# Packing a softmax bound's small matmuls into column groups, sending the result through DRAM, and moving the surrounding schedule

## The chip, the cores and the metric

The kernel runs on one core of a Trainium2 chip. The time is device time in microseconds; most executions of one kernel agree within 0.3%. Each result is a median over several executions, and ratios compare fast runs with fast runs of the kernel before that were taken in the same rounds on the same chip. The TensorE clock that was granted within a run (1.0 is full speed) is given where it matters.

## The reference

A layer norm over 2048 tokens of width 640 feeds two branches. Branch A is a recurrent attention in four segments of 512 tokens with 32 heads of 20 elements: inside a segment causal softmax attention, and across segments a memory that is read with phi(q) and updated with phi(k). Branch B is a gated feed-forward block. The output is x + A * silu(B).

```python
for s in range(N):                       # N = 4 segments
    logits = einsum('bhqd,bhkd->bhqk', qs, ks) * scale + mask
    a_dot = einsum('bhqk,bhkd->bhqd', softmax(logits), vs)
    a_mem = einsum(phi(qs), M) / (einsum(phi(qs), z) + 1e-6)
    outs.append(g * a_mem + (1 - g) * a_dot)
    M, z = M + einsum(phi(ks), vs), z + sum(phi(ks))
...
h = sigmoid(xn @ w_gate) * (xn @ w_up)   # branch B, on the same xn
return x + (o @ wo) * silu(h @ w_down)
```

## The kernel before

Softmax needs no row maximum here: from each score the kernel subtracts an upper bound, so that no exponent is positive. For query q and head h the bound is the sum over d of |q_d| times the largest |k_d| of the segment. It rides in the score matmul as one more contraction row: KT holds a row of ones beside the 20 rows of K, QT holds minus the bound beside the 20 rows of Q.

The bound itself comes from TensorE. `ik` has, for each of five chunks of 128 feature rows, the values -max|k| placed in the column of their head; `aq` is |q|. Before the change this is done for one half of the heads at a time, so twice in a segment:

```python
    def bound_mm(n, half):
        ik, aq = seg[n]["ik"], seg[n]["aq"]
        cps = ps_d.tile([16, L], F32, name="cps", tag="d")
        for i in range(3):
            nc.tensor.matmul(cps[:], lhsT=ik[:, i, :], rhs=aq[:, i, :], start=(i == 0), stop=(i == 2))
        cb = stg.tile([16, L], BF, name="cb", bufs=2)
        nc.vector.tensor_copy(cb[:], cps[:])
    def bound_dma(n, half, engs):          # SBUF to SBUF, one row per head
        for r in range(4):
            engs[r % len(engs)].dma_start(QT[32 * r + DH:32 * r + E1, 4 * half:4 * half + 4, :],
                                          cb[4 * r:4 * r + 4, :])
    def scores(unit):                      # four heads at once, in four row groups of the array
        for r in range(4):
            for (g, kb, c0, ncol, q0) in unit:
                nc.tensor.matmul(Sps[:, r, c0:c0 + ncol],
                                 lhsT=KT[32 * r:32 * r + E1, g, kb * P:(kb + 1) * P],
                                 rhs=QT[32 * r:32 * r + E1, g, q0:L], ..., tile_position=(32 * r, 0))
```

The rest of the kernel is a loop of slots, 20 to a segment and 21 in the last, numbered from 0 to 80. A slot issues one group of scores, ScalarE's exponential of them, the attention matmuls of the slot before, the planned work of that slot (projections of the next segment, phi, the memory), and as much feed-forward work (`do_gate`, `do_up`, `do_down`) as a running budget asks for. The plan of the next segment's preparation, before:

```python
        for slot, fn, c in [(9, do_K, 0), (10, do_K, 1), (11, do_K, 2), (11, do_Q, 0), (12, do_Q, 1), (13, do_Q, 2),
                            (14, do_Q, 3), (15, do_Q, 4), (16, do_K, 3), (17, do_K, 4)]:
            at(slot, GLU_NS, fn, m, c, nc.vector)
        for i in range(8):
            at(10 + i, V_NS, do_V, m, i // 2, i % 2, nc.scalar)
        ...  # phi of K at 9 to 12, memory update at 13 and 14, bounds at 15 and 19
```

In the prologue, ahead of the first scores, some gate and up pairs stand as filler for TensorE while the first Q, K and bound travel.

## Time and profile before

| | before |
|---|---|
| time, median (range) | 345.98 us (345.58 to 346.6) |
| span of the profiled execution | 344.8 us |
| TensorE busy | 333.9 us, 97% |
| VectorE, ScalarE busy | 222.2, 223.0 us |
| granted clock | 1.0 |

The line of busy times on the profile's page, where PE is TensorE's matmuls, DVE VectorE, ACT ScalarE and POOL GpSimd:

```profile
PE 333.9 (97%) x3386; PEld 184.5 (54%) x3386; DVE 222.2 (64%) x518; ACT 223.0 (65%) x220; POOL 100.8 (29%) x172
```

TensorE is the engine to relieve, and the others have slack on average.

The bound's instructions, from the view of one tile (duration minimum, median, maximum in ns; first and last start):

```profile
L287 PE MATMUL cps<-aq,ik x24: 379/379/383, 23.4 to 254.4; 128*16 128x512 bf16 x24
L289 DVE CAST cb<-cps x8: 669/678/679, 25.1 to 254.8; 16x512 bf16<-16x512 f32 x8
```

A matmul's own duration (379 ns) is not its cost, since matmuls are pipelined. Its cost is how far it pushes the next start. One unit in the loop, from the timeline (start, duration, engine):

```profile
106.99 0.81 PE L287 MATMUL cps<-aq,ik 128*16 128x512 bf16 x3
107.73 0.39 PE L471 MATMUL Sps<-QT,KT 21*128 21x512 bf16 x4
```

The three matmuls push what follows by 0.74 us. The end of the prologue, from the timeline again:

```profile
28.42 0.40 SPq L119 DMA_DIRECT2D xt<-in_A_x_dram  x1
28.93 2.57 SPq L295 DMA_DIRECT2D QT<-cb  x4
...
32.55 1.24 PE L380 MATMUL up<-xnT,Wu 128*128 128x512 bf16 x5
34.45 0.83 PE L471 MATMUL Sps<-QT,KT 21*128 21x512 bf16 x4 [0.65 <-DMA QT<-cb]
35.20 0.60 PE L371 MATMUL gp<-xnT,Wg 128*128 128x512 bf16 x2
```

TensorE waits 0.65 us for the DMA that brings the bound.

### The profile page before, as it was taken

The page shows a single profiled execution, that of the slowest core. Times are in us where ns is not written, and L with a number is a line of the kernel's source. Part 1 is how long each engine was busy: PE and PEld are TensorE (multiplying, and loading weights), DVE is VectorE, ACT ScalarE, POOL GpSimd, SP SyncE. Part 2 cuts the span into 40 slices and gives each one's busy share as a digit, 9 for nine tenths or more (in the row PEclk, how much of TensorE's full clock was granted, in tenths as well). Part 3 has the DMA queues.
Part 4 walks back from the last instruction along what each step waited for, and adds up shares of the span by engine and source line. Part 5 has one row for each costly group of instructions (what it writes and reads, how often), then busy time and mean ns, then how long its engine had stood idle before and what let it go on. Part 6 is the DMA issues. An engine that isn't in the chain of part 4 may idle for free.

```text
span 344.8 us, 8229 instructions
## 1 busy us (share of the span) xinstructions
PE 333.9 (97%) x3386; PEld 184.5 (54%) x3386; DVE 222.2 (64%) x518; ACT 223.0 (65%) x220; POOL 100.8 (29%) x172
## 2 busy tenths in 40 slices
PE   7999999999999999999999999999899999999995
PEld 3543444665554555556566455556456755545663
DVE  5374374375776777798768786878765665543354
ACT  3523676677786866766787667677956767576640
POOL 6800224223222243223232522222322232322203
PEclk9999999999999999999999999999999999999999
DMA  7977784302246614113365324024135000000002
GB/s 225 384 303 209 146 275 145 79 2 84 86 141 138 153 40 128 45 67 107 88 179 144 78 77 99 18 74 133 65 81 153 2 21 21 20 21 2 2 1 76
DMA packets 48965, 35.40 MB, mean 103 GB/s; under 512 B 25248, under 2 KB 47648, under 8 KB 48928
## 3 DMA queue, kind: packets, MB, share of 16 engines
q1 hardware_dynamic: 47616, 30.95, 32.1%
q10 hardware_dynamic: 1312, 3.93, 2.9%
q8 instruction: 26, 0.43, 0.5%
q14 instruction: 11, 0.09, 0.1%
HBM read 17.05 MB, written 11.80 MB: 84 GB/s over the span
## 4 chain that ended last, share of the span: by engine, by line
PE 84%; DVE 6%; ACT 4%; issue 2%; POOL 2%; DMA 1%; SPq 0%; DVEq 0%; ACTq 0%; POOLq 0%
PE yp L394 16%; PE up L380 13%; PE gp L371 13%; PE psq L239 11%; PE Aps L500 8%; PE Sps L471 7%; PE psv L301 5%; PE sp L418 4%; PE am L356 2%; PE cps L287 2%; ACT pt L479 1%; PE sp L452 1%; PE dm L337 1%; DMA QT<-cb 1%; DVE hT L383 1%
## 5 line engine op out<-in xcount | busy, mean ns | idle before, releaser
L479 ACT ACTIVATE pt<-Sps 128x2048 bf16<-128x2048 f32 (+1 forms) x81 | 150.3, 1855 | 36.3 <-PE Sps L471 33.1
L481 POOL TENSOR_SCALAR_AFFINE_SELECT pt<-pt 128x512 bf16<-128x512 bf16 x128 | 81.4, 651 | 227.3 <-ACT pt L479 227.3
L380 PE MATMUL up<-xnT,Wu 128*128 128x512 bf16 x240 | 59.7, 379 | 1.1 <-ACT tg L374 0.9
L371 PE MATMUL gp<-xnT,Wg 128*128 128x512 bf16 x240 | 59.7, 379 | 0.2 <-ACT V L306 0.2
L394 PE MATMUL yp<-Wd,hT 128*128 128x320 bf16 x384 | 57.5, 299 | 0.4 <-ACT oT L437 0.4
L383 DVE SCALAR_TENSOR_TENSOR hT<-tg,up 128x512 bf16<-128x512 bf16 x48 | 32.8, 683 | 37.4 <-PE up L380 27.0
L500 PEld LDWEIGHTS <-pt 128*128 128x128 bf16 x1280 | 42.7, 96 | 14.4 <-issue 3.0
L374 ACT ACTIVATE tg<-gp 128x512 bf16<-128x512 f32 x48 | 28.5, 594 | 26.1 <-PE gp L371 26.1
L500 PE MATMUL Aps<-V,pt 128*128 128x21 bf16 x1280 | 44.6, 173 | 0.0
L394 PEld LDWEIGHTS <-hT 128*128 128x128 bf16 x384 | 35.4, 97 | 15.8 <-issue 3.2
L398 DVE SCALAR_TENSOR_TENSOR aa<-t,yp 128x320 bf16<-128x320 bf16 x32 | 15.6, 488 | 34.0 <-ACT t L397 33.9
L371 PEld LDWEIGHTS <-Wg 128*128 128x128 bf16 x240 | 21.4, 97 | 23.9 <-issue 3.4
L380 PEld LDWEIGHTS <-Wu 128*128 128x128 bf16 x240 | 21.1, 97 | 24.4 <-issue 4.3
L471 PE MATMUL Sps<-QT,KT 21*128 21x128 bf16 (+3 forms) x512 | 32.8, 301 | 1.1 <-DMA QT<-cb 0.7
L301 PE MATMUL psv<-Wv,xnT 128*128 128x320 bf16 x160 | 26.5, 299 | 1.0 <-DVE ktd L244 0.8
L397 ACT ACTIVATE t<-yp 128x320 bf16<-128x320 f32 x32 | 13.9, 435 | 20.3 <-PE yp L394 19.9
L471 PEld LDWEIGHTS <-KT 21*128 21x128 bf16 x512 | 9.7, 92 | 27.6 <-issue 26.6
L239 PE MATMUL psq<-xnT,Wq 128*128 128x512 bf16 x100 | 24.3, 378 | 0.0
L239 PE MATMUL psq<-xnT,Wk 128*128 128x512 bf16 x100 | 24.3, 378 | 0.0
L306 ACT CAST V<-psv 128x320 bf16<-128x320 f32 x32 | 13.7, 427 | 15.0 <-PE psv L301 14.7
L301 PEld LDWEIGHTS <-xnT 128*128 128x128 bf16 x160 | 15.3, 98 | 11.4 <-issue 1.1
L418 PE MATMUL sp<-Wo,oT 128*128 128x320 bf16 x120 | 20.2, 298 | 0.2 <-ACT tg L374 0.2
(81 smaller groups left out, 311.5 us busy)
## 6 DMA issues: line engine op xcount, KB each, us to landing
KT<-Kd SPq DMA_DIRECT2D x32, 80.0 KB
QT<-Qd SPq DMA_DIRECT2D x32, 80.0 KB
out_dram<-xt SPq DMA_DIRECT2D x15, 160.0 KB
Wg<-in_B_w_gate_dram ACTq DMA_DIRECT2D x1, 1920.0 KB
Wu<-in_B_w_up_dram ACTq DMA_DIRECT2D x1, 1920.0 KB
xt<-in_A_x_dram SPq DMA_DIRECT2D x3, 640.0 KB
Wd<-in_B_w_down_dram SPq DMA_DIRECT2D x1, 1920.0 KB
Xd<-xn SPq DMA_DIRECT2D x12, 160.0 KB
```

The costliest lines, as they stand in the source:

```text
L239: nc.tensor.matmul(ps[:], lhsT=W[:, k, c * P:(c + 1) * P], rhs=xnT_of[n][:, k, :], start=(k == 0), stop=(k == DC - 1))
L301: nc.tensor.matmul(ps[:], lhsT=xnT_of[n][:, k, j * P:(j + 1) * P], rhs=Wv[:, k, half * HD:(half + 1) * HD], start=(k == 0), stop=(k == DC ...
L371: nc.tensor.matmul(gp[:], lhsT=Wg[:, k, f * P:(f + 1) * P], rhs=xnT_of[n][:, k, :], start=(k == 0), stop=(k == DC - 1))
L374: nc.scalar.activation(tg[:], gp[:], ACT.Tanh, scale=0.5)
L380: nc.tensor.matmul(up[:], lhsT=Wu[:, k, f * P:(f + 1) * P], rhs=xnT_of[n][:, k, :], start=(k == 0), stop=(k == DC - 1))
L383: nc.vector.scalar_tensor_tensor(out=h[:], in0=seg[n]["tg"][:], scalar=1.0, in1=up[:], op0=ALU.add, op1=ALU.mult)
L394: nc.tensor.matmul(yp[:], lhsT=s["hT"][f][:, j * P:(j + 1) * P], rhs=Wd[:, f, hs], start=(f == 0), stop=(f == FC - 1))
L418: nc.tensor.matmul(sp[:], lhsT=s["oT"][:, c, j * P:(j + 1) * P], rhs=Wo[:, c, hs], start=(c == 0), stop=(c == DC - 1))
L471: nc.tensor.matmul(Sps[:, r, c0:c0 + ncol], lhsT=KT[32 * r:32 * r + E1, g, kb * P:(kb + 1) * P], rhs=QT[32 * r:32 * r + E1, g, q0:L], star ...
L479: nc.scalar.activation(pt[:, :, 0:ntot], Sps[:, :, 0:ntot], ACT.Exp, scale=SCALE)
L481: nc.gpsimd.affine_select(out=pt[:, :, c0:c0 + P], in_=pt[:, :, c0:c0 + P], compare_op=ALU.is_ge, fill=0.0, base=0, pattern=[[0, 4], [1, P ...
L500: nc.tensor.matmul(acc["ps"][:, qb, r, :], lhsT=t[:, r, off:off + P], rhs=V[n % 2][:, kb, 4 * g + r, :], start=acc["fresh"], stop=True, sk ...
```

## The change

The intent is to spend less TensorE time on the bound. All 32 heads are now done in one unit a segment. Each chunk's stationary operand is 128 rows by 32 columns, and chunk c goes to column group c mod 3 of the array, so that three chunks can run side by side. The three column groups leave three partial sums; they are not added, but become three contraction rows of the scores (23 rows in place of 21), where the row of ones adds them. To get three rows per head into QT, the result goes through DRAM.

```diff
-    def bound_mm(n, half):
-        cps = ps_d.tile([16, L], F32, name="cps", tag="d")
-        for i in range(3):
-            nc.tensor.matmul(cps[:], lhsT=ik[:, i, :], rhs=aq[:, i, :], start=(i == 0), stop=(i == 2))
+    def bound_mm(n):
+        cps = ps_d.tile([3 * H, L], F32, name="cps", tag="d")
+        for c in range(DC):
+            i = c % 3
+            nc.tensor.matmul(cps[H * i:H * i + H, :], lhsT=ik[:, c, :], rhs=aq[:, c, :],
+                             start=(c < 3), stop=(c >= 2), tile_position=(0, H * i), skip_group_check=True)
         nc.vector.tensor_copy(cb[:], cps[:])
+        nc.sync.dma_start(Bd[n % 2][:], cb[:])
...
-            engs[r % len(engs)].dma_start(QT[32 * r + DH:32 * r + E1, 4 * half:4 * half + 4, :],
-                                          cb[4 * r:4 * r + 4, :])
+            nc.sync.dma_start(QT[32 * r + DH:32 * r + DH + 3, 4 * half:4 * half + 4, :],
+                              src[r][:, 4 * half:4 * half + 4, :])
...                                   # scores: 32 * r + E1 becomes 32 * r + DH + 3, twice
-    for f in (1, 2):                  # filler pairs after the first one
+    for f in (1, 2, 3):
...
-        for slot, fn, c in [(9, do_K, 0), (10, do_K, 1), (11, do_K, 2), (11, do_Q, 0), (12, do_Q, 1), (13, do_Q, 2),
-                            (14, do_Q, 3), (15, do_Q, 4), (16, do_K, 3), (17, do_K, 4)]:
+        for slot, fn, c in [(9, do_K, 0), (10, do_K, 1), (10, do_K, 2), (11, do_Q, 0), (11, do_Q, 1), (12, do_Q, 2),
+                            (12, do_Q, 3), (13, do_Q, 4), (13, do_K, 3), (14, do_K, 4)]:
-            at(10 + i, V_NS, do_V, m, i // 2, i % 2, nc.scalar)
+            at(12 + i, V_NS, do_V, m, i // 2, i % 2, nc.scalar)
...                                   # phi of K: slots 9-12 become 12-15; memory update: 13, 14 become 17, 18
...                                   # second half of Q spilled at 14, not 16; the bound at 15 and 16
...                                   # prologue: load of the next x issued after the bound's DMA, not before
...                                   # prologue: all K and Q projections ahead of the one bound unit
...                                   # Ind, the constant table that ik is made from: GpSimd builds one of 128x160, not two of 128x48
```

More of the change, by code (lines that the diff above doesn't have):

```diff
@@ L104 @@
     Xd = [dpool.tile([L, D], BF, name=f"Xd{i}") for i in range(2)]
+    Bd = [dpool.tile([3 * H, L], BF, name=f"Bd{i}") for i in range(2)]
     Od = [dpool.tile([L, D], BF, name=f"Od{i}") for i in range(2)]
@@ L151 @@
     nc.gpsimd.memset(KT[:].bitcast(mybir.dt.uint32), 0x3F803F80)
-    Ind = []
-    for hb in range(2):
-        t = cpool.tile([P, 3, 4, 4], F32, name=f"Ind{hb}")
-        nc.gpsimd.memset(t[:], -1.0)
-        base = 2 * hb * P - 16 * hb * DH
-        nc.gpsimd.affine_select(out=t[:], in_=t[:], compare_op=ALU.is_ge, fill=0.0, base=base,
-                                pattern=[[P, 3], [-DH, 4], [-4 * DH, 4]], channel_multiplier=1)
-        nc.gpsimd.affine_select(out=t[:], in_=t[:], compare_op=ALU.is_ge, fill=0.0, base=DH - 1 - base,
-                                pattern=[[-P, 3], [DH, 4], [4 * DH, 4]], channel_multiplier=-1)
-        Ind.append(t)
+    Ind = cpool.tile([P, DC, 4, NG], F32, name="Ind")
+    nc.gpsimd.memset(Ind[:], -1.0)
+    nc.gpsimd.affine_select(out=Ind[:], in_=Ind[:], compare_op=ALU.is_ge, fill=0.0, base=0,
+                            pattern=[[P, DC], [-DH, 4], [-4 * DH, NG]], channel_multiplier=1)
+    nc.gpsimd.affine_select(out=Ind[:], in_=Ind[:], compare_op=ALU.is_ge, fill=0.0, base=DH - 1,
+                            pattern=[[-P, DC], [DH, 4], [4 * DH, NG]], channel_multiplier=-1)
     V = [cpool.tile([P, 4, H, E1], BF, name=f"V{i}") for i in range(2)]
@@ L267, in relayout @@
             eng.dma_start(dst[32 * r:32 * r + DH, 4 * half:4 * half + 4, :], src[r])
-    def bound_q(n, half):
-        aq = stg.tile([P, 3, L], BF, name="aq")
-        U16 = mybir.dt.uint16
-        nc.vector.tensor_scalar(aq[:].bitcast(U16), seg[n]["qt"][:, 2 * half:2 * half + 3, :].bitcast(U16),
-                                0x7FFF, None, op0=ALU.bitwise_and)
-        seg[n]["aq"] = aq
-    def bound_k(n, half):
-        ik = stg.tile([P, 3, 16], BF, name="ik", bufs=2)
-        nc.vector.tensor_tensor(
-            ik[:], Ind[half][:].rearrange("p c r g -> p c (r g)"),
-            seg[n]["kabs"][:, 2 * half:2 * half + 3].unsqueeze(2).to_broadcast([P, 3, 16]), op=ALU.mult)
-        seg[n]["ik"] = ik
@@ L283, in bound_mm, with bound @@
-    def bound_mm(n, half):
-        ik, aq = seg[n]["ik"], seg[n]["aq"]
-        cps = ps_d.tile([16, L], F32, name="cps", tag="d")
-        for i in range(3):
-            nc.tensor.matmul(cps[:], lhsT=ik[:, i, :], rhs=aq[:, i, :], start=(i == 0), stop=(i == 2))
-        cb = stg.tile([16, L], BF, name="cb", bufs=2)
+    def bound(n):
+        s = seg[n]
+        ik = stg.tile([P, DC, H], BF, name="ik")
+        nc.vector.tensor_tensor(ik[:], Ind[:].rearrange("p c r g -> p c (r g)"),
+                                s["kabs"][:].unsqueeze(2).to_broadcast([P, DC, H]), op=ALU.mult)
+        aq = stg.tile([P, DC, L], BF, name="aq")
+        U16 = mybir.dt.uint16
+        nc.vector.tensor_scalar(aq[:].bitcast(U16), s["qt"][:].bitcast(U16), 0x7FFF, None, op0=ALU.bitwise_and)
+        s["bound"] = ik, aq
@@ L289, in bound_mm @@
+    def bound_mm(n):
+        ik, aq = seg[n]["bound"]
+        cps = ps_d.tile([3 * H, L], F32, name="cps", tag="d")
[3 more added lines that the diff above has]
+                             start=(c < 3), stop=(c >= 2), tile_position=(0, H * i), skip_group_check=True)
+        cb = stg.tile([3 * H, L], BF, name="cb")
         nc.vector.tensor_copy(cb[:], cps[:])
-        seg[n]["cb", half] = cb
-    def bound_dma(n, half, engs):
-        cb = seg[n]["cb", half]
+        nc.sync.dma_start(Bd[n % 2][:], cb[:])
@@ L294, in bound_dma @@
+    def bound_dma(n, half):
+        src = Bd[n % 2][:].rearrange("(i r g) n -> r i g n", i=3, r=4)
         for r in range(4):
-            engs[r % len(engs)].dma_start(QT[32 * r + DH:32 * r + E1, 4 * half:4 * half + 4, :],
-                                          cb[4 * r:4 * r + 4, :])
+            nc.sync.dma_start(QT[32 * r + DH:32 * r + DH + 3, 4 * half:4 * half + 4, :],
+                              src[r][:, 4 * half:4 * half + 4, :])
     def do_V(n, j, half, evac):
@@ L471, in scores @@
                 nc.tensor.matmul(Sps[:, r, c0:c0 + ncol],
-                                 lhsT=KT[32 * r:32 * r + E1, g, kb * P:(kb + 1) * P],
-                                 rhs=QT[32 * r:32 * r + E1, g, q0:L],
+                                 lhsT=KT[32 * r:32 * r + DH + 3, g, kb * P:(kb + 1) * P],
+                                 rhs=QT[32 * r:32 * r + DH + 3, g, q0:L],
                                  start=True, stop=True, tile_position=(32 * r, 0))
@@ L567 @@
         do_V(0, 3, half, nc.scalar)
-    for c in range(3):
+    for c in range(5):
         do_K(0, c, nc.vector)
-    spill(0, 0, nc.sync, None)
+        if c == 2:
+            spill(0, 0, nc.sync, None)
     for c in range(3):
@@ L575 @@
     relayout(0, 0, Qd, QT, nc.sync)
-    load_x(1)
-    bound_k(0, 0)
-    bound_q(0, 0)
-    do_K(0, 3, nc.vector)
-    do_K(0, 4, nc.vector)
-    bound_mm(0, 0)
-    bound_dma(0, 0, [nc.sync])
     for c in range(3, 5):
         do_Q(0, c, nc.scalar)
-    spill(0, 1, nc.sync, nc.sync)
-    bound_k(0, 1)
-    bound_q(0, 1)
-    k_tok(0)
+    bound(0)
     do_gate(0, 0)
     do_up(0, 0)
-    bound_mm(0, 1)
+    bound_mm(0)
+    bound_dma(0, 0)
+    load_x(1)
+    spill(0, 1, nc.sync, nc.sync)
+    k_tok(0)
     relayout(0, 1, Kd, KT, nc.sync)
     relayout(0, 1, Qd, QT, nc.sync)
-    bound_dma(0, 1, [nc.sync])
+    bound_dma(0, 1)
     gates()
@@ L602 @@
     GLU_NS, V_NS, TR_NS, DN_NS = DC * mm_ns(L), DC * mm_ns(HD), DC * mm_ns(P), FC * mm_ns(HD)
-    MEM_NS, C_NS = 220, 3 * mm_ns(L)
+    MEM_NS, C_NS = 220, 2 * mm_ns(L) + 200
     def segment_plan(n):
@@ L636, in segment_plan @@
         at(9, 0, new_seg, m)
-        for slot, fn, c in [(9, do_K, 0), (10, do_K, 1), (11, do_K, 2), (11, do_Q, 0), (12, do_Q, 1), (13, do_Q, 2),
-                            (14, do_Q, 3), (15, do_Q, 4), (16, do_K, 3), (17, do_K, 4)]:
+        for slot, fn, c in [(9, do_K, 0), (10, do_K, 1), (10, do_K, 2), (11, do_Q, 0), (11, do_Q, 1), (12, do_Q, 2),
+                            (12, do_Q, 3), (13, do_Q, 4), (13, do_K, 3), (14, do_K, 4)]:
             at(slot, GLU_NS, fn, m, c, nc.vector)
         for i in range(8):
-            at(10 + i, V_NS, do_V, m, i // 2, i % 2, nc.scalar)
-        for part in range(2):
-            at(9 + 2 * part, 0, phi, n, "ktok", "phik", 2 * part, 2 * part + 2)
-            at(10 + 2 * part, 0, phi_end, n, "phik", 2 * part)
-        at(13, 800, m_update, n, 0)
-        at(14, 520, m_update, n, 1)
-        at(12, 0, spill, m, 0, nc.sync, None)
-        at(13, 0, relayout, m, 0, Kd, KT, nc.sync)
-        at(14, 0, spill, m, 0, None, nc.sync)
-        at(14, 0, bound_k, m, 0)
-        at(14, 0, bound_q, m, 0)
-        at(15, C_NS, bound_mm, m, 0)
-        at(15, 0, relayout, m, 0, Qd, QT, nc.sync)
-        at(15, 0, phi, m, "qt", "phiq", 0, 2)
-        at(16, 0, phi_end, m, "phiq", 0)
-        at(16, 0, bound_dma, m, 0, [nc.sync])
-        at(16, 0, spill, m, 1, None, nc.sync)
-        at(16, 0, bound_q, m, 1)
+            at(12 + i, V_NS, do_V, m, i // 2, i % 2, nc.scalar)
+        at(11, 0, spill, m, 0, nc.sync, None)
+        at(12, 0, relayout, m, 0, Kd, KT, nc.sync)
+        at(13, 0, spill, m, 0, None, nc.sync)
+        at(14, 0, relayout, m, 0, Qd, QT, nc.sync)
+        at(14, 0, spill, m, 1, None, nc.sync)
+        at(15, 0, bound, m)
+        at(15, 0, spill, m, 1, nc.sync, None)
+        at(16, C_NS, bound_mm, m)
+        at(16, 0, phi, m, "qt", "phiq", 0, 2)
+        at(17, 0, phi_end, m, "phiq", 0)
+        at(17, 0, bound_dma, m, 0)
         at(17, 0, phi, m, "qt", "phiq", 2, 5)
         at(18, 0, phi_end, m, "phiq", 2)
-        at(18, 0, spill, m, 1, nc.sync, None)
-        at(18, 0, bound_k, m, 1)
-        at(19, C_NS, bound_mm, m, 1)
+        for part in range(2):
+            at(12 + 2 * part, 0, phi, n, "ktok", "phik", 2 * part, 2 * part + 2)
+            at(13 + 2 * part, 0, phi_end, n, "phik", 2 * part)
+        at(17, 800, m_update, n, 0)
+        at(18, 520, m_update, n, 1)
         if m < NSEG - 1:
@@ L680 @@
     for n in range(NSEG):
-        for f in range(3 if n == 0 else 0, FC):
+        for f in range(4 if n == 0 else 0, FC):
             dense.append((n, GLU_NS, lambda n=n, f=f: do_gate(n, f)))
@@ L735 @@
             relayout(n + 1, 1, Qd, QT, nc.sync)
-            bound_dma(n + 1, 1, [nc.sync])
+            bound_dma(n + 1, 1)
     for j in range(4):
```

## The prediction

> **What bounds the kernel now.** The profile page has TensorE matmuls busy 97% of the 344.8 us span, VectorE 64%, ScalarE 65%. The chain of work that ended last is 84% TensorE, and TensorE's table of waits adds up to only some 6 us, the longest 1.5 us. The granted clock is 1.0. So nearly every TensorE microsecond saved comes off the time; VectorE and DMA time count only where TensorE would have to wait for them.
>
> **What the change takes off TensorE.** The bound is now eight units of three accumulating 128x16 by 128x512 matmuls. In the timeline one unit takes 0.74 us from its first matmul to what follows (106.99 to 107.73): three times 0.216 us (five 512-column matmuls take 1.08 us in the chain) plus about 0.1. Eight units make 5.9 us. After, there are four units of five matmuls, in three column groups of the array: two rounds, if the groups run concurrently. The nearest thing in this trace is the score group: four 21-row matmuls of 512 columns in four row groups take 0.33 us until the next instruction (197.91 to 198.24); in series they would take 0.86. The Trainium skill, "TensorE: Matmul & The Clock Gate", Part 3, gives 2.38 times for three column tiles at 512 columns; no run here has shown that yet. I estimate 0.55 to 0.6 us a unit, 2.3 us in all: **3.6 us saved**. If the column groups ran in series (5 x 0.216 + 0.1 = 1.2 us a unit) only 1.2 us would be saved. A score contraction of 23 rows instead of 21 should cost nothing.
>
> **What it adds.** The bound goes through DRAM: one write of 96x512, then reads of three rows. A spill to DRAM takes about 2.5 us from its issue to the reader's (86.86 to 89.41). In the steady part this is hidden. In the prologue it is not: the first scores already wait 0.65 us for the bound's DMA (34.45). After, I put the PSUM copy's end at 29.3, the DRAM write's landing at 31.9, the reads' landing at 35.3 to 36.5; TensorE, with one more gate/up pair (2.17 us) as filler, is done at about 34.9. A wait of 0.5 to 1.5 us stays: about 0.3 us of the saving is lost.
>
> **What moves.** All K/Q projections go into slots 9 to 14 instead of 9 to 17, V and the memory update later. VectorE loses about 3.5 us of work (8 x (0.20 + 0.55 + 0.68) against an estimated 4 x (0.3 + 0.92 + 0.68)), and phi waits less for the spill. But its evacuations are packed closer, and it already slowed TensorE at 209 to 227 us. I count this as 0 +- 1.5 us.
>
> **Sum.** 345.98 - 3.6 + 0.3 = 342.7 us, range 340.2 to 345.6. Chance of faster by over 2%: 0.05; within 2%: 0.92; slower by over 2%: 0.03.
>
> **What would show it.** A bound unit advances TensorE by about 0.55 us (right), or 1.2 us (columns in series). Other TensorE instructions cost the same, scores too. The wait before the first scores is 0.5 to 1.5 us, for the bound's read. TensorE's busy time falls by about 3.5 us, its idle time is unchanged within 1.5 us. VectorE's busy time falls by about 3.5 us.
>
> **What would make it wrong.** Column groups that do not overlap, or a costly change of array mode; a first bound landing after 37 us; a VectorE backlog in slots 10 to 14, which would show as TensorE waits on K/Q/V evacuations; or a DMA queue held up so that a segment's first scores wait.

## More of the kernel before

What one engine's slack is worth has to be read stage by stage, because ScalarE must do an exponential of 1.88 us in every slot.

Last, the busy times by stage. The stretches are the prologue, the four segments (cut at the first scores of each), and the tail; the columns are the stretch, its length, then busy time and number of instructions of PE, weight loads, DVE, ACT and POOL, and at the end clock, DMA share and GB/s:

```profile
0.00:34.45 34.45, 30.83 (x161) 14.33 (x161) 17.67 (x39) 12.14 (x22) 12.84 (x36) 1.00 0.83 280
34.45:107.73 73.28, 72.80 (x754) 39.43 (x755) 42.41 (x91) 53.65 (x51) 21.32 (x34) 1.00 0.44 120
107.73:180.30 72.57, 72.57 (x790) 40.39 (x790) 56.80 (x135) 52.24 (x47) 21.17 (x34) 1.00 0.39 103
180.30:254.69 74.39, 72.12 (x776) 39.16 (x777) 58.41 (x135) 52.27 (x46) 21.77 (x34) 1.00 0.31 85
254.69:327.30 72.61, 72.61 (x789) 42.02 (x789) 37.98 (x94) 48.20 (x45) 20.23 (x33) 1.00 0.12 35
327.30:344.80 17.50, 13.02 (x125) 9.17 (x124) 8.91 (x25) 4.47 (x9) 3.43 (x3) 1.00 0.11 38
```

The third segment (180 to 255 us) is the one where TensorE stood idle for over 2 us.

## The result

| | before | after |
|---|---|---|
| time, median (range) | 345.98 us (345.58 to 346.6) | 341.47 us (341.35 to 341.66) |
| ratio | | 0.987, 95% interval 0.986 to 0.988 |
| span of the profiled execution | 344.8 us | 339.3 us |
| TensorE, VectorE busy | 333.9, 222.2 us | 330.6, 217.6 us |

A ratio is the mean time of one kernel's fast runs over the mean of the other's of the same rounds, so it is not quite the ratio of the medians. The gain is 4.5 us or 1.3%. (The spans differ by 5.5 us, because the profiled execution of the kernel before was its slowest, 346.6 us.)

After, the same four views. Busy times of the page:

```profile
PE 330.6 (97%) x3382; PEld 184.0 (54%) x3382; DVE 217.6 (64%) x506; ACT 221.5 (65%) x220; POOL 99.7 (29%) x169
```

The bound's instructions, by tile:

```profile
L281 PE MATMUL cps<-aq,ik x20: 379/389/390, 27.2 to 238.8; 128*32 128x512 bf16 x20
L284 DVE CAST cb<-cps x4: 674/680/687, 28.0 to 239.3; 96x512 bf16<-96x512 f32 x4
```

One unit in the timeline, in the loop:

```profile
94.19 0.61 PE L281 MATMUL cps<-aq,ik 128*32 128x512 bf16 x5
94.73 0.41 PE L466 MATMUL Sps<-QT,KT 23*128 23x256 bf16 x8
```

Five matmuls push the next instruction by 0.54 us, where three had taken 0.74. Note that no single matmul became shorter. The end of the prologue:

```profile
28.72 0.33 SPq L285 DMA_DIRECT2D Bd<-cb  x1
...
31.40 1.18 SPq L290 DMA_DIRECT2D QT<-Bd  x4
...
33.17 1.24 PE L375 MATMUL up<-xnT,Wu 128*128 128x512 bf16 x5
34.34 0.39 PE L466 MATMUL Sps<-QT,KT 23*128 23x512 bf16 x4
34.67 1.25 PE L366 MATMUL gp<-xnT,Wg 128*128 128x512 bf16 x5
```

No wait is left before the first scores, and the group takes 0.33 us. By stage:

```profile
0.00:34.34 34.34, 32.55 (x169) 15.42 (x169) 16.87 (x36) 12.74 (x23) 12.48 (x33) 1.00 0.77 254
34.34:106.21 71.87, 71.69 (x754) 38.85 (x754) 42.09 (x88) 53.41 (x51) 21.20 (x34) 1.00 0.55 144
106.21:179.00 72.79, 71.41 (x790) 40.47 (x790) 56.10 (x133) 51.15 (x46) 21.06 (x33) 1.00 0.38 103
179.00:249.98 70.98, 70.24 (x767) 38.23 (x767) 56.47 (x132) 51.58 (x46) 21.28 (x35) 1.00 0.32 88
249.98:321.81 71.83, 71.73 (x784) 41.87 (x784) 37.18 (x93) 48.10 (x46) 20.25 (x33) 1.00 0.13 36
321.81:339.30 17.49, 13.02 (x125) 9.17 (x124) 8.91 (x25) 4.47 (x9) 3.43 (x3) 1.00 0.11 38
```

The tail is the same to 0.01 us. The four segments take 292.85 us before and 287.47 after, 5.38 less. Of that, 2.16 us is one gate and up pair that moved into the prologue; 3.22 us is gained. The prologue ends at the same time although it has that pair more: 2.16 + 0.11 = 2.27 us gained there. Of that, 0.48 us lies before the first K matmul (14.18 against 14.66 us), and comes from a part of the change that is easily overlooked. The layer norm's `rs` is made on GpSimd, after the constant table `Ind`, and one table is done sooner than two. The first `rs` before, then after:

```profile
4.85 0.23 POOL L197 TENSOR_SCALAR rs<-mv 128x1 f32<-128x1 f32 x1
4.37 0.23 POOL L194 TENSOR_SCALAR rs<-mv 128x1 f32<-128x1 f32 x1
```

In all four profiles with two tables (the kernel before and its variants) the first `rs` starts at 4.84 or 4.85 us and the first K matmul at 14.65 or 14.66. In the changed kernel and eight of its nine variants `rs` starts at 4.36 to 4.39 and the first K matmul at 14.18 to 14.71, varying with the arrival of x; the ninth, serial96, is told of below.

So by the two traces: the bound's units give 8 x 0.74 - 4 x 0.54 = 3.8 us, the first bound's wait 1.07 us, the earlier start 0.48 us, and what is left of the 5.5 us is waits gained and lost in the loop.

**A table of slots.** To see the loop's waits I counted, from the order of instructions, how much TensorE work each slot holds, at the costs that the trace shows when nothing waits (0.216 us per 512 columns, 0.137 per 320, 0.33 for a score group and so on), leaving the bound out. A slot's excess is its length in the trace less that work. All excesses over 0.5 us, with the work in parentheses; b marks a slot with a bound unit:

```
before   0:0.53 (3.6)  15:0.71 (2.6 b)  18:0.58 (2.8)  19:0.65 (3.3 b)  35:0.70 (2.6 b)
        39:0.64 (2.8 b)  51:0.94 (5.5)  55:0.71 (2.6 b)  58:1.34 (3.8)  59:0.65 (2.2 b)
after   16:0.72 (2.6 b)  35:1.38 (1.55)  36:0.51 (3.2 b)  56:0.51 (2.6 b)  57:0.64 (3.4)
```

Before, there were waits at 0, 18, 51 and 58. After, these are gone, but a new one of 1.38 us has come at slot 35, which has only 1.55 us of TensorE work, less than one exponential. This table is an estimate, good to 0.1 or 0.2 us; it is used below for every run.

### The profile page after: what moved, and what is told of

It reads as the page before. It is cut to its first block, busy times and chain, and to the rows that moved or that the text cites. A ratio compares the mean times of both kernels' runs of the same rounds, so it can differ in the third digit from the quotient of the medians.

```text
span 339.3 us, 8214 instructions
## 1 busy us (share of the span) xinstructions
PE 330.6 (97%) x3382; PEld 184.0 (54%) x3382; DVE 217.6 (64%) x506; ACT 221.5 (65%) x220; POOL 99.7 (29%) x169
## 4 chain that ended last, share of the span: by engine, by line
PE 84%; ACT 7%; DVE 6%; POOL 1%; issue 1%; ACTq 0%; POOLq 0%
PE gp L366 15%; PE up L375 15%; PE yp L389 14%; PE psq L236 11%; PE Aps L495 8%; PE Sps L466 7%; PE sp L413 5%; PE psv L296 4%; ACT pt L474 3%; PE am L351 2%; ACT mn L312 2%; PE sp L447 1%; PE dm L332 1%; ACT V L301 1%; POOL KT L152 1%
## 5 line engine op out<-in xcount | busy, mean ns | idle before, releaser
L375 PEld LDWEIGHTS <-Wu 128*128 128x128 bf16 x240 | 21.8, 97 | 23.2 <-issue 2.8
L466 PE MATMUL Sps<-QT,KT 23*128 23x128 bf16 (+3 forms) x512 | 32.4, 301 | 1.2 <-ACT pt L474 1.0
L466 PEld LDWEIGHTS <-KT 23*128 23x128 bf16 x512 | 9.8, 92 | 27.5 <-issue 26.6
L236 PE MATMUL psq<-xnT,Wq 128*128 128x512 bf16 x100 | 23.2, 378 | 0.0
L241 DVE CAST ktd<-psq 128x512 bf16<-128x512 f32 x20 | 13.7, 683 | 8.0 <-PE psq L236 7.0
```

The costliest lines, as they stand in the source:

```text
L236: nc.tensor.matmul(ps[:], lhsT=W[:, k, c * P:(c + 1) * P], rhs=xnT_of[n][:, k, :], start=(k == 0), stop=(k == DC - 1))
L375: nc.tensor.matmul(up[:], lhsT=Wu[:, k, f * P:(f + 1) * P], rhs=xnT_of[n][:, k, :], start=(k == 0), stop=(k == DC - 1))
L466: nc.tensor.matmul(Sps[:, r, c0:c0 + ncol], lhsT=KT[32 * r:32 * r + DH + 3, g, kb * P:(kb + 1) * P], rhs=QT[32 * r:32 * r + DH + 3, g, q0: ...
```

## The experiments

The theories: (1) the column groups run side by side, and that is most of the gain; its rival, that fewer instructions and the new plan do it. (2) Filler hides the first bound's trip. (3) The new slots remove waits in the loop. All experiments are correct in their results. The first four runs of the table shared a chip and the runs of the kernel before (345.71 us there), so did the next four (346.16), the next three (345.51) and the last by itself (345.38).

| run | what it is | median us | ratio to before (95%) |
|---|---|---|---|
| serial96 | after, bound without column groups | 343.8 | 0.9942 (0.9917 to 0.9967) |
| order03142 | after, bound issued as 0,3,1,4,2 | 341.61 | 0.9883 (0.9868 to 0.9898) |
| packx4 | after, each bound unit four times | 345.76 | 1.0 (0.9985 to 1.0015) |
| filler2 | after, one filler pair less | 344.98 | 0.9971 (0.9954 to 0.9988) |
| b_filler3 | before, one filler pair more | 345.52 | 0.9988 (0.9972 to 1.0005) |
| b_sched | before, with the new slots | 350.15 | 1.0124 (1.0104 to 1.0144) |
| phi_old | after, phi of K and memory at old slots | 343.59 | 0.9932 (0.9918 to 0.9947) |
| v_old | after, V at old slots | 345.75 | 0.9996 (0.9974 to 1.0017) |
| v_even | after, V evened out | 342.23 | 0.99 (0.9882 to 0.9918) |
| filler2_v | filler2, V evened out | 343.76 | 0.9936 (0.9905 to 0.9968) |
| b_sched_q14 | b_sched, Q spilled earlier | 349.9 | 1.0122 (1.0098 to 1.0146) |
| v_spread | after, V a little evened | 341.06 | 0.9873 (0.9852 to 0.9893) |

### serial96: the bound without column groups

```diff
+    nc.gpsimd.memset(ikw[:], 0.0)        # once, in the prologue
...
-            i = c % 3
-            nc.tensor.matmul(cps[H * i:H * i + H, :], lhsT=ik[:, c, :], rhs=aq[:, c, :],
-                             start=(c < 3), stop=(c >= 2), tile_position=(0, H * i), skip_group_check=True)
+            nc.tensor.matmul(cps[:], lhsT=ik[:, 96 * c:96 * c + 96], rhs=aq[:, c, :],
+                             start=(c == 0), stop=(c == DC - 1))   # ik: zero outside the own 32 columns
```

> The changed kernel, but the five bound matmuls use a 128x96 stationary operand that is zero outside their own column group, and accumulate one after the other over the whole array: same results, same DMA, same schedule, no column groups. Theory 1 (the column groups run concurrently, and this is the main part of the gain): a unit goes from 0.54 us to about 1.1 us, the kernel is 2.0 to 2.4 us slower than the changed one, about 343.6 us. Rival (the gain is from fewer instructions and the new schedule, the groups do little): within 0.4 us of the changed kernel's 341.5 us.

Timeline of one unit:

```profile
95.03 1.24 PE L286 MATMUL cps<-aq,ikw 128*96 128x512 bf16 x5
96.20 0.30 PE L471 MATMUL Sps<-QT,KT 23*128 23x256 bf16 x4
```

The unit takes 1.17 us here and 1.08 us in the prologue (27.62 to 28.70), against 0.54. The time is 2.3 us more by the median, but the four executions fall in two pairs: 344.51 and 344.57 us with a mean granted clock of 0.995, 343.0 and 343.09 us with 0.999 and 0.997. The profiled one was of the first kind, and the stretches around 166 us show why (same columns as above; the clock is the third number from the end):

```profile
164.50:166.00 1.50, 0.50 (x10) 0.30 (x10) 1.47 (x4) 1.30 (x2) 0.45 (x1) 1.00 1.03 287
...
167.00:168.00 1.00, 1.00 (x5) 0.60 (x4) 0.86 (x3) 1.00 (x2) 0.00 (x0) 0.50 1.02 375
168.00:169.00 1.00, 1.00 (x8) 0.56 (x6) 0.00 (x0) 0.88 (x1) 0.99 (x2) 0.50 0.14 50
```

After a TensorE wait of 1.0 us the clock was halved for some 3.4 us, which costs about 1.7 us. The pair without it is 1.6 us slower than the changed kernel. Not all of that is the column groups, since the edit adds work on GpSimd in the prologue:

```profile
4.34 0.55 POOL L267 MEMSET ikw<- 128x544 bf16 x1
```

The first `rs` waits for it and starts at 4.86 us in place of 4.37, the first K matmul at 14.67 in place of 14.18: up to 0.5 us of the 1.6. So the column groups are worth some 1.1 to 1.6 us of time in this kernel (an estimate), for at least 4 x 0.54 = 2.2 us of TensorE time. The rest would have been hidden behind other waits. Theory 1 holds in that the groups run side by side. That they are most of the gain of 4.5 us is not so. My expected 2.0 to 2.4 us was too high for undisturbed executions and right only by the median.

### packx4: what one more pack costs

```diff
-        for c in range(DC):
+        for c in 4 * tuple(range(DC)):
```

> The changed kernel with each group of five bound matmuls issued four times in a row (each repetition starts the sums anew, so the result stays right): 12 packs more. Theory 1 (a pack is two rounds of 0.216 us): 12 x 0.43 = 5.2 us more, about 346.7 us. Rival (packs in series, 1.08 us each): 13 us more, about 354.4 us. If weight loads in the column groups were the limit, something between.

```profile
95.51 1.90 PE L281 MATMUL cps<-aq,ik 128*32 128x512 bf16 x20
97.34 0.41 PE L466 MATMUL Sps<-QT,KT 23*128 23x256 bf16 x8
```

Twenty matmuls push by 1.83 us, five by 0.54: three packs more cost 1.29 us, 0.43 each, which is two rounds of 0.216 us exactly. The packs run as expected. The time rose by 4.3 us and not by 5.2. The table of slots shows where the rest is: every bound slot grew by 1.3 us (16: 0.72 to 2.01, 56: 0.51 to 1.81), but the wait of 0.64 us at slot 57 and a smaller one at 17 went. TensorE had come there too early before, and waited for ScalarE; now it comes later. The same explains serial96.

A unit costs 0.54 where its two rounds are 0.43. The remaining 0.11 us, which appears once per unit and not per pack, fits what the Trainium skill says in "TensorEngine Tiling (Array Packing)", section Key Properties: changing the tiling mode drains the array. serial96 agrees: its unit, which uses the whole array, takes five rounds with nothing added in the prologue (1.08 us), and 0.09 us more only before the scores with their row groups.

### order03142: does the issue order matter?

```diff
-        for c in range(DC):
+        for c in (0, 3, 1, 4, 2):
```

> The changed kernel with the five bound matmuls issued in the order 0,3,1,4,2, so that neighbours share a column group. Theory 1 (groups overlap only between neighbouring instructions of different groups, starts in order): three rounds in place of two, a unit is 0.2 us longer, 0.9 us in all, about 342.3 us. Rival (the array looks ahead past the busy group, or the groups never overlapped): no change, 341.5 us.

```profile
94.34 0.61 PE L281 MATMUL cps<-aq,ik 128*32 128x512 bf16 x5
94.89 0.41 PE L466 MATMUL Sps<-QT,KT 23*128 23x256 bf16 x8
```

The unit takes 0.55 us, and the time is 341.61 us: no change. My expectation (starts in order, so three rounds) is refuted. The trace's own records of the unit in the prologue, with starts in us from the start of the span:

```
27.364 MATMUL cps<-aq,ik
27.371 MATMUL cps<-aq,ik
27.378 MATMUL cps<-aq,ik   $S[103]+=    (the instruction that was issued last, by its semaphore update)
27.591 MATMUL cps<-aq,ik
27.597 MATMUL cps<-aq,ik
```

Three start within 14 ns, and the one that was issued last is among them. It passed the two that had to wait for their own column group. So the groups take their work independently, and the length of a unit goes by the fullest group. Its signal did not pass them: the trace's semaphore records have it 0.64 us after the unit's start in all four units, where the changed kernel, whose signalling matmul starts 0.23 us into the unit, has it at 0.63. The modelled ends of the two that were passed are at 0.61. So matmuls started out of order here, and still the one signal at the end of the unit came after all five, as far as these four units show.

### filler2: when does the first bound land?

```diff
-    for f in (1, 2, 3):
+    for f in (1, 2):
```

> The changed kernel with two gate and up pairs as filler before the first scores in place of three (the third goes back into the loop). TensorE then reaches the first scores at about 32.2 us, and the end of its wait shows when the bound lands. Prediction as made: landing at 35.3 to 36.5, a wait of 3 to 4 us, over 344 us. Theory now (the trace has the reads issued by 32.6 and no wait at 34.3): landing at 33.2 to 34.3, a wait of 1 to 2.1 us, 342.5 to 343.6 us. Rival (landed by 32.5, the filler was not needed): 341.5 us.

```profile
31.73 1.18 SPq L290 DMA_DIRECT2D QT<-Bd  x4
33.48 1.36 PE L466 MATMUL Sps<-QT,KT 23*128 23x512 bf16 x4 [0.94 <-DMA QT<-Bd]
34.78 1.25 PE L366 MATMUL gp<-xnT,Wg 128*128 128x512 bf16 x5
```

By the records of landings the first of the four reads was in at 33.35. The score group, which needs all four in turn, took 1.30 us in place of 0.33, and the last read was in at 34.43, some 1.5 us after it was issued (32.91). The wait is 0.94 + 0.97 = 1.9 us, inside what I expected; the landing is 0.1 us later than that. In the changed kernel everything up to here is 0.3 us earlier: its last read landed at 34.14 by the same records, and TensorE arrives at 34.34. So the third pair just hides the trip through DRAM.

The time is 344.98 us, more than the expected 342.5 to 343.6, even in the three executions with a clock of 1.0 (344.43 to 345.14). The slots show the other 1.5 us or so: taking a pair out of the filler re-paces the loop, and a second slot with 1.55 us of work appears (55, with 1.38 us of excess, like slot 35). The profiled execution had half clock besides, at 239 to 243 us.

### b_filler3: the filler alone, in the kernel before

> The kernel before with one thing of the change alone: a third gate and up pair as filler before the first scores (taken from the loop). Theory 2 (the change also gains by hiding the first bound's DMA behind filler): the 0.65 us wait before the first scores goes, 345.2 to 345.4 us. Rival (moving a pair re-paces all later slots, and that matters more, as in the run with two pairs in the changed kernel, which lost 3.5 us with a wait of only 0.94): a change of another size or sign, over 0.5 us away from 345.3.

The edit is the reverse of the last one, on the kernel before. TensorE no longer waits before the first scores (35.87 us, group 0.33 us long), and up to slot 2 it has 1.17 us less excess than the profiled execution of before, as theory 2 says. But slot 39 of the loop gained an excess of 2.12 us including its bound unit (0.64 before), while the wait at slot 58 shrank. The time fell by 0.64 us against the same rounds, with a ratio whose interval just includes 1. So the local effect is shown, and the total is small and not certain: re-pacing gives back about as much as it takes.

### b_sched: the new slots alone, in the kernel before

The edit puts the changed slots of K, Q, V, phi of K and the memory update into the kernel before.

> The kernel before with the changed slots of K, Q, V, phi of K and the memory update, but its own bound in halves and its own prologue. Theory 3 (the new slots remove TensorE waits in the third segment, 1.5 us or so of before's waits at 209 to 227 us): 344 to 345 us. Rival (the slots alone gain nothing; the waits went because of the shorter bound and the pacing): 345.6 us or more.

Wrong sign: 350.15 us, 4 us slower than before. The excess is at slot 35 (1.38 us, again a slot of 1.55), 36 (1.33), and 56 (3.42, with half clock). So theory 3 in its plain form falls: the new slots are no gain by themselves. VectorE stood waiting much longer in it; this line of the table of waits (who waited for what, us in total, times, longest):

```profile
DVE qtd L318 <- DMA Qd<-qtd: 7.8, 3, 3.6
```

That is phi overwriting Q in place, which must wait until the spill of Q to DRAM has read it. It was 2.8 us before, and the changed kernel has no such line, since it spills the second half of Q two slots earlier.

### b_sched_q14: that spill earlier

```diff
-        at(14, 0, spill, m, 0, None, nc.sync)
+        at(13, 0, spill, m, 0, None, nc.sync)
+        at(14, 0, spill, m, 1, None, nc.sync)
...
-        at(16, 0, spill, m, 1, None, nc.sync)
```

The spill of Q's first half moves too, from 14 to 13, which the expectation does not say.

> The kernel before with the changed slots (350.15 us) and one more line of the change: the second half of Q is spilled at slot 14 in place of 16, before VectorE overwrites Q in place by phi. Theory 5 (the loss of 4 us is mainly VectorE standing 7.8 us in three waits for that spill's read, which also holds up ScalarE and then TensorE): the waits fall below 2 us and the time to 346 to 347.5 us. Rival (the bound in halves is too late or too much in the new slots, whatever the spill): 349 us or more.

The line is gone from the table of waits, and the time is 349.9 us. A wait of 7.8 us on VectorE cost the kernel nearly nothing. Theory 5 falls. In the undisturbed profile of this run the excess is at slots 35, 36, 56 and 57, where TensorE waits for ScalarE's tanh or exponential (longest 1.9 us, for a tanh). Why exactly those pile up with the bound in halves is left open.

### phi_old and v_old: parts of the new slots undone

In phi_old, phi of K and the memory update go back to their old slots in the changed kernel; in v_old, the V projections do (`12 + i` back to `10 + i`).

> The changed kernel with phi of K back at slots 9 to 12 and the memory update back at 13 and 14. Theory 3 (having them away from the K and Q evacuations is what keeps VectorE from holding TensorE up): 342.3 to 343.5 us, with new TensorE waits in slots 9 to 15. Rival (they don't matter there): within 0.4 us of 341.5.

> The changed kernel with the V projections back at slots 10 to 17 in place of 12 to 19. Theory 3 (V later fills slots 15 to 19, which have little other work on TensorE now that K and Q are done by 14): 342 to 343.5 us, with TensorE waiting for ScalarE's exponentials in slots 15 to 19. Rival: within 0.4 us of 341.5, since the pacing fills those slots with gate and up work anyway.

Both are slower: 343.59 us, and 345.75 us (345.03 and 345.37 in the executions with clocks of 0.997 and 0.998). phi_old is just above the 342.3 to 343.5 that was expected, and not by the way that theory 3 gave: its largest waits of TensorE are for ScalarE's exponentials (2.6 us in three, of 0.9 at most), not for VectorE. In both, four slots of the loop have 1.55 us of TensorE work (15, 35, 36, 55) where the changed kernel has one. The timeline of v_old around the first of them:

```profile
90.02 0.39 PE L466 MATMUL Sps<-QT,KT 23*128 23x512 bf16 x4
...
91.01 1.89 ACT L474 ACTIVATE pt<-Sps 128x2048 bf16<-128x2048 f32 x1
91.12 0.84 PE L296 MATMUL psv<-Wv,xnT 128*128 128x320 bf16 x5
...
92.95 0.41 PE L466 MATMUL Sps<-QT,KT 23*128 23x384 bf16 x8 [1.00 <-ACT pt L474]
```

The slot's scores are issued at 90.02, but ScalarE, busy with phi and a V evacuation, starts their exponential at 91.01 and ends it at 92.90. TensorE has done its few matmuls by 91.9, and the next scores need the same PSUM tile. So the new slots are one arrangement: with K and Q packed into slots 9 to 14, V and the memory update have to stand in 15 to 19, or those slots run empty.

### v_even, filler2_v and v_spread: filling the short slots

If short slots are what is left, evening them out should gain. Only the V slots differ: 14, 15, 16, 16, 17, 17, 18, 19 in v_even; 13, 14, 15, 16, 18, 18, 19, 19 in filler2_v (on top of filler2); 13, 14, 15, 15, 16, 17, 18, 19 in v_spread.

> The changed kernel with the V projections at slots 14, 15, 16, 16, 17, 17, 18, 19 in place of 12 to 19. Counted from the order of instructions, the changed kernel has one slot with only 1.55 us of TensorE work (slot 35 of 80), less than one exponential of 1.88 us, and the trace has TensorE's 1.0 us wait just after it; the variant with V at the old slots has four such slots and lost 4.3 us. Theory 4 (short slots make TensorE wait for ScalarE, and evening them out is worth their shortfall): no slot under 2.2 us here, the 1.0 us wait goes, 340.2 to 341.0 us. Rival (the waits come from the total load of VectorE and ScalarE in slots 12 to 19, which stays): 341.3 us or more.

> The changed kernel with two filler pairs (the run that took 344.98 us with a wait of 0.94 us for the bound) and V at slots 13, 14, 15, 16, 18, 18, 19, 19, chosen so that no slot is short (two of 1.55 us before). Theory 4: the wait for the bound's DMA stays at about 0.9 us, the loop's waits mostly go, 342 to 343 us. Rival (with two pairs the rest of the loss is from something else): 344.3 us or more.

> The changed kernel with V at slots 13, 14, 15, 15, 16, 17, 18, 19: two V units in slot 15, slots 16 to 19 as in the changed kernel. The last run (V more even still) did take away the wait of 1.38 us after the short slot 35, but new waits of about the same sum came at slots 18, 36, 56 and 57, where it had put more V evacuations on ScalarE beside phi. Theory 4b (both count: short slots, and ScalarE's load in slots 16 to 18): here slot 35 has 2.2 us instead of 1.55 and slots 16 to 18 carry the same as in the changed kernel, so 0.3 to 0.8 us is gained, 340.7 to 341.2 us. Rival (waits only move): 341.4 us or more.

v_even has no slot under 2.2 us, and the excess at slot 35 fell from 1.38 to 0.30 us, as theory 4 says. But the time is 342.23 us, not better. New excesses stand at 18 (0.47), 36 (0.99), 56 (1.12) and 57 (1.10): there it has two V evacuations a slot on ScalarE, beside phi. Two lines of its table of TensorE's waits:

```profile
PE dm L332 <- ACT tg L369: 1.0, 1, 1.0
PE up L375 <- DVE hT L378: 0.5, 1, 0.5
```

filler2_v came out in two pairs again: 342.09 and 343.29 us at clocks of 0.998 and 0.999, 344.23 and 344.66 at 0.995. Against filler2's 344.4 to 345.1 at full clock, some 2 us are gained, and its short slots are gone; the wait for the bound stayed (1.24 us, then 1.0 within the score group). The median of all four, 343.76, lies between the expected 342 to 343 and the rival's 344.3, so this run alone decides nothing.

v_spread has 341.06 us (340.79 to 341.25), and the excess at slot 35 is half (0.70), at 57 too (0.36), while slot 15 has a new one (0.70). Its ratio to before, 0.9873, is that of the changed kernel, 0.987, within either interval. A gain over the changed kernel is not shown, though its slowest execution was under the other's fastest: the two were on different chips.

## Why the prediction was right

The predicted time was 342.7 us with a range of 340.2 to 345.6, and 341.47 was measured. Point by point:

- **The bound's units.** Predicted 0.55 to 0.6 us each; measured 0.54. Predicted 3.6 us of TensorE time saved; 3.8 by the units' lengths in the traces. TensorE's busy time fell by 3.3 us (predicted about 3.5). That the column groups run side by side is shown by serial96 (1.08 us a unit) and packx4 (0.43 us a pack). They are 2.2 of the 3.8 us; the rest comes of five matmuls a segment in one unit in place of six in two. What prediction and expectations overlooked is that saved TensorE time is not all saved: packx4 adds 5.2 us of it and 4.3 of time, and serial96 some 1.1 to 1.6 of time for at least 2.2. The Trainium skill's figure of 2.38 times for three column tiles ("TensorE: Matmul & The Clock Gate", Part 3) was the right order: by packx4, five matmuls in three groups go 1.08 / 0.43 = 2.5 times as fast as in series, and a single unit, with its 0.11 us, 1.08 / 0.54 = 2.0 times.
- **23 contraction rows in place of 21** cost nothing: the score matmuls' median is 298 ns in both traces.
- **The first bound's trip.** "A wait of 0.5 to 1.5 us stays" is the step that failed. None stayed. The mis-sized term was the landing of the reads, put at 35.3 to 36.5; the last landed at 34.14. The PSUM copy ended at 28.70 (predicted 29.3) and the write to DRAM landed at 31.38 (predicted 31.9), and from there the reads took 2.8 us, where the prediction had 3.4 to 4.6. The wait that was there before was also larger than I read it, 1.07 us and not 0.65, as it goes on inside the score group. And the prediction passed over the order of the DMAs: before, the load of the next x stood ahead of the bound's and landed at 34.12; after, it stands behind. What this order, the filler and the other route are each worth is not isolated; b_filler3 shows that filler alone hides the wait of the kernel before. So up to the second slot the change gained 2.27 + 0.42 = 2.7 us, where 0.9 - 0.3 = 0.6 was predicted; 0.48 us of it is GpSimd's one table in place of two, which the prediction did not see. The rest of the loop gained 3.22 - 0.42 = 2.8 us, where the sum had 2.7. That this agrees so closely is in part luck: waits came and went there, and the profiled execution of before was its slowest. The trip of the first bound (1.07 us gained, where 0.3 lost was predicted) and the table are together more than the 1.2 us between the predicted 3.3 us and the measured 4.5.
- **What moves: 0 +- 1.5 us.** This was right as a sum, in part by luck, and says little, since it is a balance of large parts. Undone one by one they cost 2.1 us (phi and memory) and 4.3 us (V, by medians), and put into the kernel before they cost 4 us. TensorE's idle time fell by 2.2 us (10.9 to 8.7), more than the 1.5 predicted, by the stages: 1.8 us in the prologue and 1.5 in the third segment, against 1.4 us more in the second.
- **VectorE** lost 4.6 us of work, 3.5 predicted. It was right that phi would wait less for the spill, and b_sched_q14 shows that this wait was worth almost nothing.
- **What would make it wrong** named VectorE's backlog in slots 10 to 14. The waits that came were in slots 15 to 17, and for ScalarE.
- **A slip in reading.** The "longest 1.5 us" of TensorE's waits before is the total of two; the longest single one is 1.2 us. Nothing in the sum rests on it.

What stays open: why the new slots cost the kernel before 4 us, with the bound in halves; and how much of the gain over before each part holds by itself, since the parts do not add up (any shift of one pair re-paces all later slots).

## What to carry to other kernels

When several small stationary operands stand in a row on a busy TensorE, give them different column groups and let a later contraction add the partial sums: the cost then goes by the fullest group. In a loop of slots where ScalarE has a fixed job in each, look for slots with less TensorE work than that job, not at average load; taking work off TensorE pays only until such a slot, and moving one piece of filler re-paces all that follow. And read a wait in the profile together with the length of the group behind it, since a group fed by several DMAs hides its later waits.

## What the Trainium skill lacked or had wrong

- "TensorE: Matmul & The Clock Gate", Part 3, The mechanism, says of matmuls: "strict FIFO, no reordering" in start and end. With column groups the order of starts does not hold here: in order03142 the matmul issued last started at 27.378 us, before two issued ahead of it (27.591 and 27.597), and the issue order 0,3,1,4,2 was as fast as 0,1,2,3,4 (0.55 and 0.54 us a unit). What it says of the end is not contradicted: the signal of that matmul came at 0.64 us, after the modelled ends of the other two (0.61).
- The same place says in its list that weight loads overlap running matmuls only when the row group differs, though the paragraph above that list also allows it for the background weight buffer. In the changed kernel's records all five weight loads of a unit start within 19 ns (27.221 to 27.240 us), all with the same 128 rows and three different column groups, while the first three matmuls start at 27.223 to 27.230 and take 390 ns each. So the list is too strict.
- The same page, Part 1, "HAM oscillation", ties the half clock to TensorE gaps of over about 3.4 us; for a second case it speaks of shorter gaps, without a length. Here waits of 1.0 to about 2 us were followed by half clock, for 3.41 us each time in the records (serial96, filler2, filler2_v and b_sched, once each in the profiled execution), costing about 1.7 us by estimate; that length is the window which the page gives. Other waits, as the one of 1.0 us in the changed kernel and one of 1.94 in b_sched_q14, were not followed by it, and it comes in some executions of a kernel and not in others.
- "TensorEngine Tiling (Array Packing)" gives no figure for the drain at a change of tiling mode. A unit here cost 0.11 us more than its two rounds, and in the prologue its first matmul came another 0.09 us late (27.223 us, 0.31 after the one before it, where a round is 0.216); serial96's whole-array unit had neither there.
- No page gives SyncE's time to issue one DMA: the four that bring the bound into QT took 2.57 us to issue before (SBUF to SBUF, each 4 pieces of 1 KB into one row) and 1.18 us after (from DRAM, each 3 rows of 4 KB). The source alone does not set it, as the write of 96 rows from SBUF to DRAM took 0.33 us to issue; which of the differences does is not shown.
